# The last group's downward product: a bank of its own for the third step, the last step in two halves

## The chip, the cores and the metric

The kernel runs on one core of one Trainium2 chip. The metric is the device time of one execution in microseconds (us); of several runs the median is given.

## The reference

Attention with a sliding window and a few global keys gives 3072 tokens of 512 numbers. A router sends each token to one of 8 experts, and the expert's two-layer network makes the output. Only the second half matters here:

```python
logits = x @ w_gate                      # x: 3072 x 512, w_gate: 512 x 8
expert_idx = np.argmax(logits, axis=1)
gate_w = probs[np.arange(N), expert_idx]
for e in range(E):
    mask = expert_idx == e
    h = np.maximum(x[mask] @ w1[e], 0.0)     # 512 -> 1024
    out[mask] = gate_w[mask, None] * (h @ w2[e])   # 1024 -> 512
```

Everything is float32.

## The kernel before, in words

The attention writes each token's row, with its gate and its number, to a region of DRAM per expert. The experts then run as groups, in the order 0, 8 (the late tokens of expert 0), 1, ..., 7. `group(p)` records the work of a group. Group 7 is the last, and the only one that the change touches.

A group has up to 512 tokens, in two halves of up to 256. TensorE (PE) multiplies the weights, as stationary operand, by tokens, as moving operand; the number of moving columns is chosen at run time among 17 forms (128 to 256), and PE branches into the code of one form (L277, `emit_forms`). In the runs here the last group takes the form with 136 columns. Each layer is done by Strassen's scheme in Winograd's form: `seven` returns seven products, with sums on VectorE (DVE) and copies on ScalarE (ACT) around them. A product of the downward layer is 8 matmuls of 128x128 by 128x136; each leaves two records in the profile[...].

`seven` works with PSUM banks. There are two sets of three banks, `(0, 1, 2)` and `(3, 4, 7)`, which alternate from call to call: X, Y, W are this call's, X2, Y2, W2 those of the other set. Banks 6 and 5 (`tbanks`, handed out in turn by `bank()`) take the transposes of the output. The downward call of the last group (`half` given) runs its steps in the order one, two, four, five, six, three, last:

- `one`: b11 x a11 into X; ACT copies it to p1 (L898).
- `two`: t2 x s[1] into Y; DVE makes u2 = p1 + Y (L902).
- `four`: t3 x s[2] into Y; DVE makes u3 = u2 + Y (L913).
- `five`: t1 x s[0] into W; DVE makes c22 = u3 + W (L929).
- `six`: t4 x a22 into Y; DVE makes c21 = u3 + Y (L934).
- `three`: b21 x a12 added into X; ACT copies X to c11 (L909). In its middle `half()` turns and gates the blocks 1 and 3, which c21 and c22 complete.
- `last`: b22 x s[3] added into W; DVE makes c12 = u2 + W (L939).

`y_out` turns a block of 128 tokens with four transposes on PE (L849), one for each tile of 128 outputs, scales it by the gates on ACT (L852) or DVE (L854) into `self.y[j]`, and sends the rows to their places in the output with an indirect DMA of GpSimd (POOL, L860). Tiles 0 and 1 of blocks 0 and 2 come from c11, tiles 2 and 3 from c12. Blocks 1 and 3 are sent from within the program of the groups. Blocks 0 and 2 of the last group are turned and gated after it (L1404, L1405) and sent later, after a branch that every engine takes:

```python
    with tc.If(f.loads["redo"] > 0):      # L1801: a general version, for inputs outside the limits
        ...
    for j in (0, 2):
        d = ex.send(nc.gpsimd, order[-1], j)
```

Ahead of this branch SyncE (SP) collects a signal from every engine, and answers with one that POOL waits for before the sends (L216, `play`). The branch skips the general version's code.

`Flow` records operations in the order in which they are called, which is the order on each engine, and derives the semaphores: a PSUM bank is guarded as a whole, so a product into a bank waits for every earlier reader of it. The waits are put ahead of an instruction by L238.

Of the kernel before, what the change touches and what calls it, by code (L numbers as in the profile page):

```python
# [16 lines left out]
AF = mybir.ActivationFunctionType  # L17
ALU = mybir.AluOpType
# [644 lines left out]
class Experts:  # L663
# [163 lines left out]
    def bank(self):  # L827
        self.tp ^= 1
        return self.psum[:, self.tbanks[self.tp], :].rearrange("p (c t) -> p c t", c=4)
# [12 lines left out]
                lambda: V.tensor_tensor(sx[:, 2], a11, a21, ALU.subtract),  # L842
                lambda: V.tensor_tensor(sx[:, 3], a12, sx[:, 1], ALU.subtract)]

    def y_out(self, g, j, on="act", send=True):
        f, k, pt = self.f, self.keep, self.bank()
        hh, bb = (j % 2, j // 2) if g != self.E else (0, j)
        for c in range(4):
            f.pe.transpose(pt[:, c, :], self.yt[:, c, hh, ts(bb, 128)], k["ident"][:])  # L849
        y = self.y[j].rearrange("p (c t) -> p c t", c=4)  # L850
        if on == "act":
            f.act.activation(y, pt, AF.Copy, bias=0.0, scale=k["gt"][:, g, j, 0:1])  # L852
        else:
            f.dve.tensor_scalar(y, pt, k["gt"][:, g, j, 0:1], None, ALU.mult)  # L854
        if send:
            self.send(f.pool, g, j, _r=[k["to"][:, g, j:j + 1], self.y[j]], _w=[f"out{g}.{j}"])

    def send(self, pool, g, j, **kw):

# [13 lines left out]
            if half and t == 0:  # L873
                half()

    def seven(self, c, a, s, cols, order, dst, act, half=None, common=False):


        f, V = self.f, self.f.dve
        X, Y, W = self.sets[self.turn]  # L880
        X2, Y2, W2 = self.sets[self.turn ^ 1]
        some, past = slice(0, self.COMMON if common else 256), slice(self.COMMON, 256)
        p1, u2, u3 = self.p1[self.turn], self.u2[self.turn], self.u3[self.turn]
        self.turn ^= 1

        def bank(b):
            return self.psum[:, b, :].rearrange("p (t c) -> p t c", t=2)

        def mm(b, wq, xq, fresh, half=None, cut=slice(0, 256)):
            self.product(b, [c[wq][:, k, cols] for k in order], [xq[:, k, :] for k in order], fresh, half, cut)  # L890

        def relu(d):
            if act:
                f.act.activation(d, d, act)  # L894

        def one():
            mm(X, "b11", a["a11"], True, cut=some)
            f.act.copy(p1[:, :, some], bank(X)[:, :, some])  # L898

        def two():  # L900
            mm(Y, "t2", s[1], True, cut=some)
            V.tensor_tensor(u2[:, :, some], p1[:, :, some], bank(Y)[:, :, some], ALU.add)  # L902

        def three():
            mm(X, "b21", a["a12"], False, half, some)
            if act:
                f.act.activation(dst["c11"][:, :, some], bank(X)[:, :, some], act)  # L907
            else:
                f.act.copy(dst["c11"], bank(X))  # L909

        def four():
            mm(Y, "t3", s[2], True, cut=some)
            V.tensor_tensor(u3[:, :, some], u2[:, :, some], bank(Y)[:, :, some], ALU.add)  # L913

        def rest():
            T = self.tbanks[self.tp ^ 1]
            mm(X2, "b11", a["a11"], True, cut=past)
            f.act.copy(p1[:, :, past], bank(X2)[:, :, past])
            mm(Y2, "t2", s[1], True, cut=past)
            V.tensor_tensor(u2[:, :, past], p1[:, :, past], bank(Y2)[:, :, past], ALU.add)  # L920
            mm(W2, "b11", a["a11"], True, cut=past)
            mm(W2, "b21", a["a12"], False, cut=past)
            f.act.activation(dst["c11"][:, :, past], bank(W2)[:, :, past], act)
            mm(T, "t3", s[2], True, cut=past)
            V.tensor_tensor(u3[:, :, past], u2[:, :, past], bank(T)[:, :, past], ALU.add)

        def five():
            mm(W, "t1", s[0], True)
            V.tensor_tensor(dst["c22"], u3, bank(W), ALU.add)  # L929
            relu(dst["c22"])  # L930

        def six():
            mm(Y, "t4", a["a22"], True)
            V.tensor_tensor(dst["c21"], u3, bank(Y), ALU.add)  # L934
            relu(dst["c21"])

        def last():
            mm(W, "b22", s[3], False)
            V.tensor_tensor(dst["c12"], u2, bank(W), ALU.add)  # L939
            relu(dst["c12"])  # L940

        if half:
            return [one, two, four, five, six, three, last]
        if common:
            return [one, two, three, four, lambda: [rest(), five()], six, last]
        return [one, two, three, four, five, six, last]
# [24 lines left out]
    def down(self, e, half=None):  # L971

        c, h, yt = self.quarters(e, False), self.h, self.yt
        a = dict(a11=h[:, 0:4, 0], a12=h[:, 4:8, 0], a21=h[:, 0:4, 1], a22=h[:, 4:8, 1])
        s = [self.sh[:, j] for j in range(4)]
        dst = dict(c11=yt[:, 0:2, 0], c12=yt[:, 2:4, 0], c21=yt[:, 0:2, 1], c22=yt[:, 2:4, 1])
        return self.seven(c, a, s, slice(0, 256), (0, 1, 2, 3), dst, None, half)


    def plain(self, e, slack):  # L980
# [23 lines left out]
def kernel(  # L1004
# [51 lines left out]
    ident, iota_p, col, before, ones, rev8, ebase, base_e, tokid = (  # L1056
        keep[nm] for nm in ("ident", "iota_p", "col", "before", "ones", "rev8", "ebase", "base_e", "tokid"))
# [7 lines left out]
    with ExitStack() as stack:  # L1065
# [6 lines left out]
        f = Flow(tc)  # L1072
# [3 lines left out]
        ex = Experts(f, dict(moe_w1=moe_w1, moe_w2=moe_w2, xs=xg_dram, XW=XW, REGION=NTOK, out=out), psum, keep,  # L1076
                     (Arena(big, 0, WSET), Arena(big, WSET, WSET)), Arena(big, 2 * WSET, 22560 - 2 * DM), small[:, 0:XW], ylast[:])
        N, V = at.N, f.dve
# [25 lines left out]
        whole, half = slice(0, NBLK), NBLK // 2  # L1104
# [150 lines left out]
        order = [0, E, *range(1, E)]  # L1255
# [145 lines left out]

        for p in range(len(order)):
            group(p)
        for j, on in ((0, "act"), (2, "dve")):  # L1404
            ex.y_out(order[-1], j, on, send=False)  # L1405
        landing = f.play(later={f"out{order[-1]}.{j}" for j in (1, 3)})


    def anything(ctx):
# [372 lines left out]
        with tc.manual_schedule(engines={PE}):  # L1782
            for j in range(XB - 1):
                gather(j)
            for j in range(2):
                fetch(j)
            x_in(0)
            for j in range(JT):
                up(j)
                if j + 1 < JT:  # L1790
                    x_in(j + 1)
                if j:
                    down(j - 1)
                if j + XB - 1 < JT:
                    gather(j + XB - 1)
                if j + 2 < JT:
                    fetch(j + 2)
            down(JT - 1)
# [44 lines left out]
```

## Time and profile before

| what | us |
|---|---|
| median of 3 runs | 501.79 (500.29 to 501.93) |
| the profiled execution's own time | 500.38 |
| its span, first to last instruction | 498.5 |
| PE busy / DVE busy / ACT busy / POOL busy | 474.9 / 356.1 / 173.2 / 164.7 |
| granted clock of PE, mean | 0.991 of full speed |

The profile is of one execution; times within it count from its first instruction. The 1.9 us between its span and its own time lie around the span. A busy PE is not PE at its peak. A row of the time-line that merges several records starts with the first and ends with the last. In the rows of a branch or a semaphore the letter q marks the engine's own queue, as in POOLq; these rows are not counted as busy.

The downward call of the last group begins at about 469 us; its last matmul starts at 483.74, the last gate ends at 486.53, the two last sends start at 488.03 and 489.31, their data have landed by 492.6, and the span ends at 498.5.

### The profile page before, as it was taken

The numbers are of one execution on the slowest core, as the hardware profiler recorded it, in microseconds if no ns is written. First come the engines' busy times: TensorE is split into PE (matmuls) and PEld (weight loads), VectorE is DVE, ScalarE is ACT, GpSimd is POOL, SyncE is SP. The second block draws the span as 40 slices with busy tenths as digits, with TensorE's granted clock in tenths as the row PEclk, the third lists the DMA queues.
The fourth block names the chain that finished last, engine by engine and source line by source line (L and its number), as shares of the span: only waits on it lengthen the run. The fifth ranks groups of instructions, "written<-read, shape, count | busy, mean of one in ns | idle before, by whom it ended". The sixth has DMA issues, their size and how long they took to land. (4 is left out here: it accounts for less than half of the span.)

```text
span 498.5 us, 10842 instructions
## 1 busy us (share of the span) xinstructions
PE 474.9 (95%) x4413; PEld 450.0 (90%) x4413; DVE 356.1 (71%) x646; ACT 173.2 (35%) x309; POOL 164.7 (33%) x192
## 2 busy tenths in 40 slices
PE   7999999999997999999999999999999999999990
PEld 6888878878886899999999999999999999999880
DVE  6466766897888883766876886877877667778830
ACT  5656555654654230323123223214213204303310
POOL 2653576567774053303013113204304303003011
PEclk9999999999999999999999999999999999999996
DMA  9999999997624438896874773756666568001000
GB/s 175 215 246 237 213 237 267 244 212 188 149 87 86 172 129 189 215 265 131 189 214 111 192 217 102 172 181 156 157 204 146 121 175 239 0 1 66 3 26 30
DMA packets 120093, 79.26 MB, mean 159 GB/s; under 512 B 86170, under 2 KB 103066, under 8 KB 120020
## 3 DMA queue, kind: packets, MB, share of 16 engines
q1 hardware_dynamic: 112482, 63.52, 56.4%
q0 software_dynamic: 6480, 14.45, 8.1%
q8 instruction: 52, 0.85, 0.7%
q10 hardware_dynamic: 1058, 0.26, 0.2%
q14 instruction: 21, 0.17, 0.1%
HBM read 61.39 MB, written 23.71 MB: 171 GB/s over the span
## 5 line engine op out<-in xcount | busy, mean ns | idle before, releaser
L870 PE MATMUL psum<-arena 128*128 128x208 f32 (+5 forms) x1776 | 290.8, 325 | 1.0 <-DVE arena L902 0.8
L870 PEld LDWEIGHTS psum<-arena 128*128 128x128 f32 x1776 | 285.5, 190 | 2.6 <-DVE arena L902 1.3
L860 POOL DMA_INDIRECT out_dram<-arena,to x16 | 22.5, 1403 | 171.9 <-ACT arena L852 147.2
L529 DVE TENSOR_TENSOR arena<-psum,arena 128x1024 f32<-128x1024 f32 x40 | 48.3, 1219 | 29.4 <-PE psum L519 29.4
L537 ACT ACTIVATE arena<-arena 128x1024 f32<-128x1024 f32 (+1 forms) x48 | 47.4, 988 | 47.5 <-DVE arena L529 40.2
L543 POOL TENSOR_TENSOR arena<-arena 128x512 f32<-128x512 f32 x40 | 51.9, 1300 | 30.9 <-ACT arena L537 30.5
L894 ACT ACTIVATE arena<-arena 128x512 f32<-128x512 f32 x48 | 30.2, 630 | 53.4 <-DVE arena L929 27.5
L519 PE MATMUL psum<-arena 64*128 64x128 f32 x704 | 46.4, 280 | 1.6 <-ACT arena L505 1.6
L519 PEld LDWEIGHTS psum<-arena 64*128 64x128 f32 x704 | 41.8, 187 | 5.2 <-issue 2.5
L556 PE MATMUL psum<-arena 128*64 128x128 f32 x704 | 43.7, 276 | 0.3 <-issue 0.3
L898 ACT COPY arena<-psum 128x512 f32<-128x512 f32 (+1 forms) x24 | 13.5, 561 | 81.8 <-PE psum L870 81.7
L556 PEld LDWEIGHTS psum<-arena 128*64 128x64 f32 x704 | 37.9, 137 | 2.9 <-issue 0.6
L783 POOL DMA_INDIRECT xg_dram<-small,pad x24 | 23.4, 975 | 50.9 <-ACT arena L907 40.0
L655 POOL DMA_INDIRECT xg_dram<-arena,slot_i x24 | 25.4, 1058 | 21.9 <-DVE arena L939 16.2
L913 DVE TENSOR_TENSOR arena<-arena,psum 128x512 f32<-128x512 f32 (+1 forms) x24 | 15.8, 659 | 23.3 <-PE psum L870 21.9
L939 DVE TENSOR_TENSOR arena<-arena,psum 128x512 f32<-128x512 f32 x24 | 16.5, 688 | 17.8 <-PE psum L870 17.8
L934 DVE TENSOR_TENSOR arena<-arena,psum 128x512 f32<-128x512 f32 x24 | 16.5, 688 | 14.7 <-PE psum L870 11.5
L929 DVE TENSOR_TENSOR arena<-arena,psum 128x512 f32<-128x512 f32 x24 | 16.5, 688 | 13.5 <-PE psum L870 12.6
L860 POOL DMA_INDIRECT out_dram<-ylast,to x17 | 17.0, 1000 | 21.0 <-ACT ylast L852 13.1
L741 DVE TENSOR_TENSOR arena<-arena 128x1024 f32<-128x1024 f32 x16 | 21.1, 1321 | 1.3 <-issue 1.1
L902 DVE TENSOR_TENSOR arena<-arena,psum 128x512 f32<-128x512 f32 (+1 forms) x24 | 15.7, 656 | 8.5 <-PE psum L870 8.0
L738 DVE TENSOR_TENSOR arena<-arena 128x1024 f32<-128x1024 f32 x16 | 19.4, 1211 | 1.9 <-DMA arena<-in_moe_w_dram 1.9
(162 smaller groups left out, 541.8 us busy)
## 6 DMA issues: line engine op xcount, KB each, us to landing
arena<-in_moe_w_dram SPq DMA_DIRECT2D x64, 512.0 KB
arena<-xg_dram SPq DMA_DIRECT2D x64, 128.0 KB
arena<-in_v_dram SPq DMA_DIRECT2D x24, 256.0 KB
arena<-in_q_dram SPq DMA_DIRECT2D x23, 256.0 KB
arena<-in_k_dram SPq DMA_DIRECT2D x23, 256.0 KB
xg_dram<-arena SPq DMA_DIRECT2D x2, 1032.0 KB
xg_dram<-arena,slot_i POOLq DMA_INDIRECT x24, 5.5
xg_dram<-small,pad POOLq DMA_INDIRECT x24, 8.2
```

The lines of the kernel that those rows point to most:

```text
L519: f.pe.matmul(self.psum[:, 2 * g + a, c:c + P], lhsT=kt[r, m, :], rhs=qt[r, m, :], start=True, stop=True, skip_group_check=True)
L529: f.dve.tensor_tensor(e, s, self.bias[:, g, :, 1:3, :].rearrange("p h k c -> p h (k c)"), ALU.add)
L537: f.act.activation(e, e, AF.Exp)
L543: f.pool.tensor_tensor(self.es[n % 3][:, g], e[:, :, 0:P], e[:, :, P:2 * P], ALU.add)
L556: f.pe.matmul(po[r, m, :], lhsT=self.v[(n - ab) % 6][:, 2 * m + a, :], rhs=self.e[n % 2][:, m // 2, 2 * a + m % 2, P * ab:P * ab + P], sta ...
L655: self.f.pool.indirect_dma_start(out=self.xs[:], out_offset=bass.IndirectOffsetOnAxis(ap=k["slot_i"][:, b % 2, u:u + 1], axis=0), in_=self ...
L738: return [lambda: V.tensor_tensor(c["t3"], c["b22"], c["b12"], ALU.subtract), lambda: V.tensor_tensor(c["t1"], c["b12"], c["b11"], ALU.sub ...
L741: lambda: V.tensor_tensor(c["t4"], c["b21"], c["t2"], ALU.subtract)]
L783: self.f.pool.indirect_dma_start(out=self.xs[:], out_offset=bass.IndirectOffsetOnAxis(ap=self.keep["pad"][:, g, j:j + 1], axis=0), in_=sel ...
L860: return pool.indirect_dma_start(out=self.out[:], out_offset=bass.IndirectOffsetOnAxis(ap=self.keep["to"][:, g, j:j + 1], axis=0), in_=sel ...
L870: f.pe.matmul(self.psum[:, bank, 256 * t + cut.start:256 * t + cut.stop], lhsT=w[k][:, ts(t, 128)], rhs=x[k][:, cut], start=(fresh and t = ...
L894: f.act.activation(d, d, act)
```

## The change

In the last group's downward call alone:

- `four_end` puts the product t3 x s[2] into X2, and DVE makes u3 from there.
- `five_end` is `five`, and DVE then adds W to u2 as well. `last_end` therefore needs nothing of W.
- `last_end` puts b22 x s[3] into two fresh banks, the first 128 outputs into Y2 and the second into W2. After the first half DVE adds 128x256; then the tiles 0 and 1 of blocks 0 and 2 are turned into the banks 6 and 5 and gated (block 0 on ACT, block 2 on DVE). After the second half DVE adds the other 128x256; the tiles 2 and 3 are turned into W and X2 and gated.
- `y_out` is split into `y_turn` and `y_gate`. The calls of `y_out` for blocks 0 and 2 after the groups go; their transposes now lie inside each of PE's 17 forms.

The sends stay where they were.

```diff
-    def y_out(self, g, j, on="act", send=True):
+    def y_out(self, g, j, on="act"):
+        pt = self.bank()
+        self.y_turn(g, j, pt, range(4))
+        self.y_gate(g, j, pt, slice(0, 4), on)
+        self.send(self.f.pool, g, j, _r=[self.keep["to"][:, g, j:j + 1], self.y[j]], _w=[f"out{g}.{j}"])
+    def y_turn(self, g, j, pt, tiles):
         hh, bb = (j % 2, j // 2) if g != self.E else (0, j)
-        for c in range(4):
+        for c in tiles:
+            self.f.pe.transpose(pt[:, c, :], self.yt[:, c, hh, ts(bb, 128)], self.keep["ident"][:])
+    def y_gate(self, g, j, pt, tiles, on):
+        f, gate = self.f, self.keep["gt"][:, g, j, 0:1]
+        y = self.y[j].rearrange("p (c t) -> p c t", c=4)[:, tiles]
...
+        def four_end():
+            mm(X2, "t3", s[2], True)
+            V.tensor_tensor(u3, u2, bank(X2), ALU.add)
+        def five_end():
+            five()
+            V.tensor_tensor(u2, u2, bank(W), ALU.add)
+        def last_end():
+            blocks = (0, "act"), (2, "dve")
+            first, second = [self.bank(), self.bank()], [self.psum[:, b, :].rearrange("p (c t) -> p c t", c=4)
+                                                         for b in (W, X2)]
+            for t, b in enumerate((Y2, W2)):
+                for k in order:
+                    f.pe.matmul(self.psum[:, b, 0:256], lhsT=c["b22"][:, k, ts(t, 128)], rhs=s[3][:, k, :],
+                                start=(k == 0), stop=True, skip_group_check=True, _dyn=True)
+                V.tensor_tensor(dst["c12"][:, t], u2[:, t], self.psum[:, b, 0:256], ALU.add)
+                if t == 0:
+                    for pt, (j, on) in zip(first, blocks):
+                        self.y_turn(end, j, pt, (0, 1))
+                        self.y_gate(end, j, pt, slice(0, 2), on)
+            for tile in (2, 3):
+                for pt, (j, on) in zip(second, blocks):
+                    self.y_turn(end, j, pt, (tile,))
+            for pt, (j, on) in zip(second, blocks):
+                self.y_gate(end, j, pt, slice(2, 4), on)
...
         if half:
-            return [one, two, four, five, six, three, last]
+            return [one, two, four_end, five_end, six, three, last_end]
...
         for p in range(len(order)):
             group(p)
-        for j, on in ((0, "act"), (2, "dve")):
-            ex.y_out(order[-1], j, on, send=False)
```

## The prediction

> **What bounds the kernel now.** I start with the page's head and its busy shares.
>
> ```profile
> span 498.5 us, 10842 instructions
> PE 474.9 (95%) x4413; PEld 450.0 (90%) x4413; DVE 356.1 (71%) x646; ACT 173.2 (35%) x309; POOL 164.7 (33%) x192
> ```
>
> TensorE (PE) is the bound of the whole span, but the change touches only the last downward stage, so I read the end. The time-line of the last 30 us, one engine at a time, shows the place where PE rests inside that stage (columns: start, length, engine, line, operation, tiles, shape, count, idle time before and what ended it):
>
> ```profile
> 470.73 1.96 PE L870 MATMUL psum<-arena 128*128 128x136 f32 x15
> 473.54 1.66 PE L870 MATMUL psum<-arena 128*128 128x136 f32 x12 [0.85 <-DVE arena L902]
> ...
> 472.80 0.69 DVE L902 TENSOR_TENSOR arena<-arena,psum 128x512 f32<-128x512 f32 x1
> 473.40 1.22 DVE L741 TENSOR_TENSOR arena<-arena 128x1024 f32<-128x1024 f32 x1
> ```
>
> The reader is to see that `two`'s sum (L902) reads bank Y from 472.80 to 473.49 and that PE starts `four`, which overwrites Y, only at 473.54. From there PE runs without a pause to the end of `last`. The end of the stage and the output:
>
> ```profile
> 481.35 0.75 DVE L854 TENSOR_SCALAR arena<-psum,gt 128x512 f32<-128x512 f32 x1 [1.26 <-PE psum L849]
> ...
> 482.38 0.97 POOL L860 DMA_INDIRECT out_dram<-arena,to  x1 [22.25 <-DVE arena L854]
> 483.66 0.98 POOL L860 DMA_INDIRECT out_dram<-arena,to  x1 [0.30 <-issue]
> ...
> 484.06 0.69 DVE L939 TENSOR_TENSOR arena<-arena,psum 128x512 f32<-128x512 f32 x1 [1.96 <-PE psum L870]
> 484.80 0.88 PE L849 MATMUL psum<-ident,arena 128*128 128x128 f32 x6 [0.56 <-DVE arena L939]
> 485.33 0.69 ACT L852 ACTIVATE ylast<-psum,gt 128x512 f32<-128x512 f32 x1 [2.54 <-PE psum L849]
> 485.78 0.75 DVE L854 TENSOR_SCALAR ylast<-psum,gt 128x512 f32<-128x512 f32 x1 [1.04 <-PE psum L849]
> 488.03 0.97 POOL L860 DMA_INDIRECT out_dram<-ylast,to  x1 [3.39 <-remote]
> 489.31 0.98 POOL L860 DMA_INDIRECT out_dram<-ylast,to  x1 [0.30 <-issue]
> ```
>
> The last gate ends at 486.53, yet the first of the last two sends starts at 488.03. Does the gate or POOL set that start? The chain that ended last, and the instructions of the branch (L1801), answer:
>
> ```profile
> 486.10 0.91 another core or an unknown queue
> 487.01 0.10 POOLq L1801
> 487.11 0.03 issue
> 487.14 0.04 POOLq L860
> ...
> L1801 POOLq EVENT_SEMAPHORE  x6: 17/30/43, 485.6 to 486.1; - x6
> L1801 POOLq COMPARE_BRANCH  x1: 50/50/50, 482.9 to 482.9; - x1
> L1801 SPq COMPARE_BRANCH  x1: 50/50/50, 486.8 to 486.8; - x1
> ```
>
> The chain never reaches the gate. POOL branches at 482.95, right after it has issued the send of block 3; nothing of its queue runs for 2.67 us; from 485.62 it works through bookkeeping of semaphores (one step of 0.97 us), is at the send's waits at 487.23 and starts at 488.03. The other way in, last gate 486.53, SP's collection of the engines' signals, SP's release at 486.74, was there 0.49 us sooner. So **two ways end close together, and POOL's is the later**: gate of block 3 (481.35) to branch to send. Behind the sends, POOL's final drain and the closing barrier follow:
>
> ```profile
> L1838 POOLq DRAIN  x3: 40/188/8636, 488.3 to 497.9; - x3
> ```
>
> **What the skill says.** Three places bear on this. "PSUM — Partial Sum Buffer", section "PSUM bank collisions raise a hardware error": a bank must be guarded as a whole between engines, not by address. The trace agrees with the cost of that: PE waits 0.85 us for L902's read of Y. "Runtime: NRT & Kernel Launch", section "Instruction fetch mechanics": a taken branch whose target lies outside the fetched pages forces a DMA fetch. The trace agrees: after L1801's branch the queues resume 2.67 (POOL), 2.93 (SP), 2.98 (ACT) and 3.24 us (DVE) later. "Perfetto Trace Analysis", section on SWDGE instructions: a POOL DMA's bar ends with the writing of descriptors, not with the data. Here the bar is 0.97 us and landing comes 3.4 us after issue.
>
> **The change part by part.**
>
> 1. `four` goes to X2. That bank's last readers belong to the upward stage and are long done. The last matmul of `two` starts at 472.41 and the first of `four` at 473.54: 1.13 us where the rhythm is 0.116, so 1.01 us goes. The first matmul after that wait also delays its successor by 0.10 (0.22 from start to start). Sum **1.11 us**. What is late next: `four` needs the second half of s[2] (L955, ended 472.18) and its own 5th record at 472.99: no wait, at most 0.06 for a satisfied one, as in `two` (0.175 once instead of 0.116). Range 1.05 to 1.11. Then u3's sum: PE would be ready for it at 474.58, DVE is in L741 until 474.62; nobody needs u3 before `five` ends at 476.4, so nothing.
>
> 2. `u2 + W` is a new DVE sum of 128x512: 0.69 by row L929, 0.60 from start to start behind another. It sits between c22 (shifted: 476.50) and c21, whose product ends for 478.29. It is over at 477.79, 0.50 ahead: no cost; without that cover, c21 and the turn of blocks 1 and 3 would be late by what exceeds 0.50.
>
> 3. With 1 and 2 all of `five`, `six`, `three`, the turns of blocks 1 and 3, their gates, POOL's two sends and POOL's branch move forward by 1.11: branch at 481.84. POOL's instructions, sends and descriptors are the same in number and order; one block jump goes (below 0.1). After the same 2.67 of fetch and the same 2.40 of bookkeeping and issue the send starts at 486.91 instead of 488.03, provided SP's release is in by 486.12 instead of 487.23.
>
> 4. The halves of `last`: no matmul more or less (8), no transpose more or less (8). New shapes: DVE sums of 128x256, estimate 0.42 from 128x512 (0.69), 128x416 (0.58) and 128x96 (0.255); DVE gate of 128x256, estimate 0.48 (0.75 less 0.27); ACT gate of 128x256, 0.38 to 0.45 by row L994 (0.384 for that shape). Shifted, `last` starts at 480.89 and half one ends at 481.82. Turns of tiles 0 and 1 need c11 (ACT copy, shifted end 481.67): just met. Four turns x 0.109 to 482.26, second half to 483.19, its sum 483.39 to 483.81, two turns of tile 2 within that cover, two of tile 3 from 483.87, DVE's gate 484.42 to **484.90**. Before: 486.53. This way shortens by 1.63, that is 0.52 more than step 1. It was not the later way, so the 0.52 is worth **nothing**: the release comes at 485.10, 1.0 us ahead of POOL.
>
> 5. PE's jump to the end of the form moves behind the last turns, where it was hidden under matmuls (481.8). Cost 0.30 by its row:
>
> ```profile
> L277 PEldq COMPARE_BRANCH  x13: 292/303/909, 252.4 to 481.8; - x13
> ```
>
> It lies beside the gate's 0.48 and in the 1.0 of slack: nothing.
>
> Sum: 1.11 less 0 to 0.06, and 0 to 0.1 back: **1.1 us** less, at the end of the span. In the profiled execution: 500.38 - 1.1 = 499.3. That execution stands 1.41 under the median of the runs (501.79); the four times known (500.29, 500.38, 501.79, 501.93) average 501.10, which gives 500.0, and the median gives 500.7. I take 500.2.
>
> Unknown costs, both sides: POOL's fetch after the branch. The placement of its code changes by an instruction or so. If the target fell into pages already there, POOL would gain at most until the release governs, step 4's 1.63 and the 0.49 together: 2.1 us. If it takes as long as the slowest seen (PE's 3.6), 0.95 is lost again: 0.15 gained.
>
> **The rivals.**
>
> - The gain of both ways counts, or the fetch shortens: 1.6 to 2.1 us, 499.0 to 499.5 against 501.1. For it: the diff works mostly on the gate's way. Against it: the chain goes through POOL.
> - Nothing arrives (about 501.1): POOL's branch, or the drain after it, is tied to something that doesn't move. For it: the drain of 8.6 us ends 4.3 us after the last data landed, and no view says what it waits for. Against it: every step from the gate of block 3 on follows its predecessor without slack.
> - Slower: PE's jump (step 5) now has no matmuls in front to hide it. If it costs a fetch as L1801's do (2.7 to 3.6), PE's signal comes at 483.9 + 3.6 = 487.5, the release at 487.7 and the send 0.5 us later than before: 501.6 against 501.1. It loses from about 3.1 us of jump on. Against it: 13 such jumps took 0.29 to 0.91, with a prefetch hint ahead of each. A second wait of that kind on the other engines' jumps would make it worse, to +1.6.
> - The change might not remove the wait at all, if X2 were still held: its last reader (L907 of the upward stage) ended at 465.39, those of Y2 and W2 (L934, L939) by 469.65, so no.
>
> **How the numbers follow.** POOL's way, 1.1 us: 0.66. More, 1.6 to 2.1: 0.17. Nothing: 0.09. Slower: 0.08. A difference of 0.3% (1.5 us) is about what a measurement of this kernel can tell from no change, and the runs shown spread over 1.6 us. The likeliest case, 0.22%, lies under that bound; because the median before is at the upper end of its times I give half of it to either side: faster 0.33 + 0.17 = 0.50, same 0.33 + 0.09 = 0.42, slower 0.08. The range goes from 2.1 off the mean of the four, less 0.3 of scatter (498.7), to no gain at the upper median (501.8).
>
> **What would show it.** Right: PE has no pause before `four`; the sends of blocks 1 and 3 start 1.1 us sooner; the last gates end about 484.9; the last two sends start about 486.9, again 5 us after POOL's branch; the chain still runs through POOL. Wrong: a pause ahead of the turns of blocks 1 and 3 (step 2), a send that starts right after SP's release (step 4 counts), a POOL fetch unlike 2.67, a jump of PE over 1 us.

## The result and the profile after

The changed kernel takes 500.18 us (median of 20 runs, 498.97 to 502.26) against 501.75 (20 runs) for the kernel before. The ratio is 0.9973, with a 95% interval of 0.9961 to 0.9985: 1.35 us less, between 0.75 and 1.96. Ratios and intervals, here and below, are worked out from the fast runs alone (executions more than 1.5% above the fastest are left out), and are not quotients of the medians, which lie 1.57 us apart here. The prediction was 1.1 us less.

The profiled execution of the kernel after took 502.08 us itself, at the upper end of its runs. It reached the last downward call 2.75 us later than the profiled execution before. The change edits nothing ahead of that point, and the point moves between executions of one and the same kernel: 472.31 here and 470.41 in a second profile of the kernel after; over the 14 profiles of this study, of all versions, it lies anywhere from 469.56 to 474.44. So I compare from a mark inside the stage. The mark is the start of the last group's first sum of the hidden layer on DVE, 469.56 before and 472.31 after; **the tail** is the time from there to the end of the span: 28.97 us before, 27.86 after, 1.11 less. To set a time of the profile after beside one of before, take 2.75 off.

The page's head and its busy shares:

```profile
span 500.2 us, 10823 instructions
PE 475.9 (95%) x4413; PEld 451.1 (90%) x4413; DVE 359.6 (72%) x649; ACT 173.6 (35%) x310; POOL 164.7 (33%) x192
```

PE has its 4413 records as before; DVE has 3 instructions more (one sum, and the last sum and gate in halves). The shares say nothing of the gain.

The time-line of PE (start, length, engine, line, operation, shape, count, idle time before and what ended it):

```profile
469.81 12.11 PE L876 MATMUL psum<-arena 128*128 128x136 f32 x102
...
486.61 0.44 PE L854 MATMUL psum<-ident,arena 128*128 128x128 f32 x2 [0.30 <-DVE arena L961]
```

The reader is to see one unbroken row from ahead of the mark to the turn of blocks 1 and 3: the pause of 0.85 us before `four` is gone. The only pause left is the 0.30 before the last two turns. The time-line of DVE:

```profile
475.55 0.69 DVE L908 TENSOR_TENSOR arena<-arena,psum 128x512 f32<-128x512 f32 x1
...
477.40 0.69 DVE L945 TENSOR_TENSOR arena<-arena,psum 128x512 f32<-128x512 f32 x1
...
479.86 0.68 DVE L950 TENSOR_TENSOR arena<-arena,psum 128x512 f32<-128x512 f32 x1
481.04 0.69 DVE L940 TENSOR_TENSOR arena<-arena,psum 128x512 f32<-128x512 f32 x1 [0.50 <-PE psum L876]
482.98 0.75 DVE L862 TENSOR_SCALAR arena<-psum,gt 128x512 f32<-128x512 f32 x1 [1.26 <-PE psum L854]
484.76 0.42 DVE L961 TENSOR_TENSOR arena<-arena,psum 128x256 f32<-128x256 f32 x1 [1.03 <-PE psum L959]
485.27 0.48 DVE L862 TENSOR_SCALAR ylast<-psum,gt 128x256 f32<-128x256 f32 x1
...
487.08 0.48 DVE L862 TENSOR_SCALAR ylast<-psum,gt 128x256 f32<-128x256 f32 x1 [0.53 <-PE psum L854]
```

L945 is u3 from the new bank, L950 the added sum u2 + W: after it DVE still waits 0.50 us for `six` before c21 (L940). The gate of block 3 starts at 482.98, on the clock of before at 480.23 against 481.35. The last gate ends at 487.56, that is 484.81 against 486.53. The time-line of POOL, the end of the chain, and the branch (now L1834):

```profile
484.01 0.97 POOL L866 DMA_INDIRECT out_dram<-arena,to  x1 [21.14 <-DVE arena L862]
485.29 0.97 POOL L866 DMA_INDIRECT out_dram<-arena,to  x1 [0.30 <-issue]
489.68 0.97 POOL L866 DMA_INDIRECT out_dram<-ylast,to  x1 [3.41 <-remote]
490.95 0.97 POOL L866 DMA_INDIRECT out_dram<-ylast,to  x1 [0.30 <-issue]
```

```profile
487.75 0.91 another core or an unknown queue
488.66 0.10 POOLq L1834
488.76 0.03 issue
488.80 0.04 POOLq L866
```

```profile
L1834 POOLq EVENT_SEMAPHORE  x6: 17/30/43, 487.3 to 487.7; - x6
L1834 POOLq COMPARE_BRANCH  x1: 50/50/50, 484.6 to 484.6; - x1
L1834 SPq COMPARE_BRANCH  x1: 50/50/50, 487.8 to 487.8; - x1
```

The sends of blocks 1 and 3 come 1.11 us sooner, the last two 1.10 sooner, and the chain still goes through POOL's bookkeeping after its branch, not through a gate. The last gate is over at 487.56 and SP's release in at 487.78; the first of the last sends starts only at 489.68. I read "remote" as the releaser of that send, behind which the profile names no engine, as POOL's own bookkeeping of semaphores; where SP's release decides, the releaser reads "SPq", as some experiments show.

### The profile page after: what moved, and what is told of

Read it like the earlier page. It is cut to its first block, busy times and chain, and to the rows that moved or that the text cites. A ratio compares the mean times of both kernels' runs of the same rounds, so it can differ in the third digit from the quotient of the medians.

```text
span 500.2 us, 10823 instructions
## 1 busy us (share of the span) xinstructions
PE 475.9 (95%) x4413; PEld 451.1 (90%) x4413; DVE 359.6 (72%) x649; ACT 173.6 (35%) x310; POOL 164.7 (33%) x192
## 5 line engine op out<-in xcount | busy, mean ns | idle before, releaser
L556 PE MATMUL psum<-arena 128*64 128x128 f32 x704 | 45.0, 281 | 0.3 <-issue 0.3
L556 PEld LDWEIGHTS psum<-arena 128*64 128x64 f32 x704 | 39.1, 140 | 2.9 <-issue 0.6
L940 DVE TENSOR_TENSOR arena<-arena,psum 128x512 f32<-128x512 f32 x24 | 16.5, 688 | 14.5 <-PE psum L876 14.3
L741 DVE TENSOR_TENSOR arena<-arena 128x1024 f32<-128x1024 f32 x16 | 22.9, 1429 | 1.3 <-issue 1.1
L738 DVE TENSOR_TENSOR arena<-arena 128x1024 f32<-128x1024 f32 x16 | 19.4, 1210 | 2.1 <-DMA arena<-in_moe_w_dram 2.1
```

Of the source, the lines that this page charges most:

```text
L556: f.pe.matmul(po[r, m, :], lhsT=self.v[(n - ab) % 6][:, 2 * m + a, :], rhs=self.e[n % 2][:, m // 2, 2 * a + m % 2, P * ab:P * ab + P], sta ...
L738: return [lambda: V.tensor_tensor(c["t3"], c["b22"], c["b12"], ALU.subtract), lambda: V.tensor_tensor(c["t1"], c["b12"], c["b11"], ALU.sub ...
L741: lambda: V.tensor_tensor(c["t4"], c["b21"], c["t2"], ALU.subtract)]
```

## Experiments

Two theories stood at the start. **P**: the end follows POOL's branch, which follows the gate of block 3, so only the new bank (and u2 + W, which lets the last step do without W) brings anything. **G**: the end follows the last gate, so the halves bring their share. All tails in us from the mark. "POOL's way" is worked out from each trace: start of POOL's branch, 0.05 for it (0.07 with the hint), the gap after it, and 2.40 from POOL's next instruction to the send. "Release's way" is SP's release plus 0.79. The 2.40 and the 0.79 are read from these same traces: the first is the same in all seven of before, after (twice) and experiments 1, 2, 5 and 7, the second is seen alone in experiment 6. Experiments 3 to 6 and 11 are one execution each, and only their traces are used. The names are those of the experiments below.

| kernel | mark | tail | POOL's branch | gap after it | last gate ends | SP's release | POOL's way | release's way | first of the last sends |
|---|---|---|---|---|---|---|---|---|---|
| before | 469.56 | 28.97 | 13.39 | 2.62 | 16.97 | 17.17 | 18.46 | 17.96 | 18.46 |
| after | 472.31 | 27.86 | 12.27 | 2.64 | 15.25 | 15.47 | 17.36 | 16.26 | 17.37 |
| after, again | 470.41 | 28.15 | 12.26 | 2.94 | 15.25 | 15.46 | 17.65 | 16.25 | 17.65 |
| 1 bank alone | 469.63 | 28.00 | 12.26 | 2.79 | 15.85 | 16.05 | 17.50 | 16.84 | 17.50 |
| 2 halves alone | 469.94 | 29.18 | 13.39 | 2.84 | 16.38 | 16.59 | 18.68 | 17.38 | 18.68 |
| 3 two passes more | 470.10 | 28.74 | 12.27 | 2.72 | 16.29 | 17.46 | 17.44 | 18.25 | 18.24 |
| 4 five passes more | 471.01 | 30.16 | 12.27 | 2.95 | 17.85 | 18.88 | 17.67 | 19.67 | 19.67 |
| 5 gate 3 twice | 469.58 | 28.65 | 13.02 | 2.68 | 15.25 | 15.46 | 18.15 | 16.25 | 18.15 |
| 6 without two sends | 472.85 | 26.23 | -12.08 | - | 15.25 | 15.46 | - | 16.25 | 16.25 |
| 7 outer halves | 472.02 | 27.41 | 11.91 | 2.55 | 15.18 | 15.39 | 16.91 | 16.18 | 16.91 |
| 9 hint | 469.72 | 26.73 | 12.40 | 0.43 | 15.25 | 15.46 | 15.30 | 16.25 | 16.24 |
| 10 hint, bank alone | 471.73 | 27.32 | 12.40 | 0.43 | 15.85 | 16.05 | 15.30 | 16.84 | 16.82 |

In every row the send starts at the later of the two ways, within 0.02 us. From that send to the end of the span it is 10.5 us in every row but that of experiment 6 (9.98).

**1. The bank alone.** `four_end` stays; `five_end`, `last_end` and the turns between the halves go.

```diff
-            return [one, two, four_end, five_end, six, three, last_end]
+            return [one, two, four_end, five, six, three, last]
...
+        for j, on in ((0, "act"), (2, "dve")):
+            pt = ex.bank()
+            ex.y_turn(order[-1], j, pt, range(4))
+            ex.y_gate(order[-1], j, pt, slice(0, 4), on)
```

> The change's first half alone: four goes to X2, but last adds into W and is summed, turned and gated whole, after the groups, as before. I measure the tail: from the first of the last group's h-sums on DVE (469.56 in the profile before, 472.31 in the profile after) to the end of the span. It was 28.97 us before and is 27.86 after. Theory P (the end follows POOL's branch, which follows the gate of block 3): tail 27.86, all of the gain, although the last gate ends some 0.6 us later in the tail than after the whole change; time about 1.1 us under before. Rival G (the end follows the last gate): tail about 28.47, half of the gain.

Measured: 501.06 us (22 runs) against 502.58 (43 runs), ratio 0.9975 (0.996 to 0.9991): 1.26 us less, between 0.45 and 2.01. The tail is 28.00. From the time-lines of DVE and of POOL:

```profile
484.73 0.75 DVE L862 TENSOR_SCALAR ylast<-psum,gt 128x512 f32<-128x512 f32 x1 [1.04 <-PE psum L854]
```

```profile
487.13 0.97 POOL L866 DMA_INDIRECT out_dram<-ylast,to  x1 [3.56 <-remote]
```

The last gate ends 0.60 later from the mark than in the kernel after (15.85 against 15.25), yet the send is only 0.13 later, and the gap after POOL's branch is 0.15 longer (2.79 against 2.64). P holds: the bank brings the whole gain.

**2. The halves alone.** `four` goes back to Y.

```diff
-            return [one, two, four_end, five_end, six, three, last_end]
+            return [one, two, four, five_end, six, three, last_end]
```

> The change's second half alone: four goes to Y as before, so PE waits for the sum of two; the last product is in halves in two banks, with the turns and gates between. Theory P: tail 28.97 as before, no gain, though the last gate ends 0.6 us sooner. Rival G: tail about 28.36, a gain of 0.6 us.

Measured: 501.61 us (22 runs) against 502.58, ratio 0.9984 (0.9959 to 1.0009): no difference that these runs could tell. The tail decides: 29.18, as long as before plus the 0.22 by which the gap after POOL's branch is longer. From the time-lines of PE and of POOL:

```profile
473.91 4.32 PE L876 MATMUL psum<-arena 128*128 128x136 f32 x35 [0.85 <-DVE arena L908]
```

```profile
488.62 0.97 POOL L866 DMA_INDIRECT out_dram<-ylast,to  x1 [3.62 <-remote]
```

With `four` in Y the pause of 0.85 is back to the hundredth. The release comes 0.58 sooner than before (16.59 against 17.17) and nothing follows from it: G falls here, since it wanted 28.36.

**3. Two more passes of the last DVE gate**, to eat up the slack of the gate's way without touching POOL's.

```diff
             for pt, (j, on) in zip(second, blocks):
-                self.y_gate(end, j, pt, slice(2, 4), on)
+                for _ in range(1 if on == "act" else 3):
+                    self.y_gate(end, j, pt, slice(2, 4), on)
```

> The changed kernel, with the last gate of block 2 (128x256 on DVE, 0.48 us, 0.40 from start to start) computed three times in a row, to the same result: the last gate and SP's release come 0.8 us later. Theory P: the release still comes 0.3 us ahead of POOL, tail 27.86 as after the change. Rival G: tail 28.66.

Measured: tail 28.74, not 27.86. The time-lines of DVE and of POOL:

```profile
484.87 1.52 DVE L862 TENSOR_SCALAR ylast<-psum,gt 128x256 f32<-128x256 f32 x3 [0.53 <-PE psum L854]
```

```profile
488.34 0.97 POOL L866 DMA_INDIRECT out_dram<-ylast,to  x1 [4.30 <-SPq L216]
```

My size was wrong, not the theory. Each pass waits for the one before it and costs 0.52, so the gate ends 1.04 later; and the release then came 1.17 us after the gate's end, where it is 0.22 in the kernel after. Between them stands DVE's jump to the end of the form, which has a record of 0.05 us but after which DVE's queue came back only 1.3 us later. So the release moved by 1.99, past POOL's way (17.44 against 18.25), and the send started 0.78 after it. The releaser now reads "SPq L216": this is what a send that waits for the gates looks like.

**4. Five more passes**, well past the slack.

```diff
-                self.y_gate(end, j, pt, slice(2, 4), on)
+                for _ in range(1 if on == "act" else 6):
+                    self.y_gate(end, j, pt, slice(2, 4), on)
```

> The same with the last gate of block 2 computed six times: 2.0 us later. Theory P: the slack of 1.08 is used up and the release becomes the later way; tail 27.86 + 2.0 - 1.08 = 28.8. Rival G: tail 29.86. If the end hung on neither: 27.86.

Measured: tail 30.16, again more than expected, and for the same two reasons: the release moved by 3.41, to 18.88.

```profile
490.68 0.97 POOL L866 DMA_INDIRECT out_dram<-ylast,to  x1 [5.72 <-SPq L216]
```

The send starts 0.79 after it. From experiment 3 to this one release and send both move by 1.42 to 1.43: once the release is the later way, the end follows it one for one. Of the 3.41, the tail shows 2.30; the kernel after therefore had 1.11 to spare, against the 1.10 between its two ways in the table.

**5. The gate of block 3 twice**, in the kernel after: the other way in made longer.

```diff
-        self.y_gate(g, j, pt, slice(0, 4), on)
+        for _ in range(2 if on == "dve" else 1):
+            self.y_gate(g, j, pt, slice(0, 4), on)
```

> The changed kernel, with the gate of block 3 (128x512 on DVE) computed twice in a row, to the same result. DVE is idle for about 1.0 us behind it, so the second pass delays only POOL's send of block 3 and its branch, by 0.67 us. Theory P: tail 27.86 + 0.67 = 28.53. Rival G: tail 27.86, since the gates of blocks 0 and 2 don't move.

Measured: tail 28.65, 0.79 longer. The second pass waits for the first and costs 0.75; POOL's branch moves from 12.27 to 13.02, and the gap after it is 0.04 longer. The last gate ends at 15.25 in both.

```profile
487.73 0.97 POOL L867 DMA_INDIRECT out_dram<-ylast,to  x1 [4.18 <-remote]
```

The same engine and the same kind of instruction cost 0.75 here at full price and in experiment 3 were free up to the slack. That is P.

**6. Without the sends of blocks 1 and 3**, so that POOL reaches its branch long before.

```diff
         self.y_gate(g, j, pt, slice(0, 4), on)
+        if g == 7:
+            return
```

> The changed kernel without the two sends of blocks 1 and 3 of the last group: those rows of the output are not written. POOL has then nothing to wait for ahead of its branch and goes through it long before. Theory P, with its second part (behind POOL's way stands SP's release, some 1.05 us sooner): the first of the last two sends starts about 0.8 us behind SP's release instead of 1.9, tail 26.8. Rival G, or an end that hangs on something else than POOL's branch: tail 27.86.

Measured: tail 26.23; the first of the last sends starts at 16.25. From the instructions of the branch and the time-line of POOL:

```profile
L1836 POOLq COMPARE_BRANCH  x1: 50/50/50, 460.8 to 460.8; - x1
```

```profile
489.10 0.97 POOL L868 DMA_INDIRECT out_dram<-ylast,to  x1 [25.69 <-SPq L216]
```

With POOL out of the way the release governs, and its price of 0.79 from release to send is seen alone. The tail is 0.57 shorter than I expected, as from send to end it is 9.98 instead of 10.5. POOL's final drain took 8.47 us instead of 8.63, and the rest lies behind the drain; why two sends less shorten them isn't shown.

**7. The outer blocks' turns in halves as well**, so that the gate of block 3 ends sooner: `six_end` turns and gates tiles 2 and 3 of blocks 1 and 3 right after c21, `three_end` the tiles 0 and 1 where `half()` stood.

```diff
-            return [one, two, four_end, five_end, six, three, last_end]
+            return [one, two, four_end, five_end, six_end, three_end, last_end]
...
+        def six_end():
+            six()
+            self.early = [self.bank(), self.bank()]
+            for pt, (j, on) in zip(self.early, ((1, "act"), (3, "dve"))):
+                self.y_turn(end, j, pt, (2, 3))
+                self.y_gate(end, j, pt, slice(2, 4), on)
```

> A version meant to be faster by theory P: the changed kernel, and the blocks 1 and 3 are now treated as the change treats 0 and 2. Their tiles 2 and 3 (from c22) are turned right behind six and gated in halves of 128x256, their tiles 0 and 1 (from c21) are turned after three of the four matmuls of three's first half, into Y2 and W2. The gate of block 3 ends about 0.65 us sooner, block 1's about 0.4 sooner, and POOL issues the second send at best 0.55 behind the first: branch and end 0.38 us sooner. Theory P: tail 27.48. Rival G: 27.86 (the gates of blocks 0 and 2 stay).

Measured: 501.19 us (22 runs) against 502.86 (43 runs), ratio 0.9973 (0.9956 to 0.999); tail 27.41. POOL's branch is 0.36 sooner than in the kernel after and the gap 0.09 shorter, and the tail is 0.45 shorter. Halves pay where they stand ahead of the branch. The time itself can't be told from that of the kernel after.

**8. The kernel after a second time**, in the same comparison, unchanged.

> The changed kernel once more, on the same chip as the version before it, for a comparison of the two and for a second profile: tail 27.86 if it does not depend on the execution; the time about 1.1 us under before.

Measured: 501.74 us (22 runs) against 502.86, ratio 0.9987 (0.9965 to 1.0009); tail 28.15. Every time up to POOL's branch repeats within 0.01 us, but the gap after the branch was 2.94 instead of 2.64. The gain in the tail is 0.82 here, and by these runs alone it could also be none at all.

**9. A hint for POOL's branch**, set ahead of all of POOL's work (0.7 us into the span), some 480 us before the branch. If the gap is the fetch of the target's instructions, it should go, and the release become the later way. First one execution, then 22 against 43 of the kernel before:

```diff
+        self.tc.mark_branch_hint_location("redo", "LikelyTaken", [mybir.EngineType.Pool])
...
-    with tc.If(f.loads["redo"] > 0):
+    with tc.If(f.loads["redo"] > 0, label="redo"):
```

> The changed kernel with a prefetch hint for POOL's branch at L1834, set at the start of POOL's program, as PE's forms have one for their jump (0.30 us each in the profile). Theory P: if the hint is used, the 2.6 to 2.9 us between POOL's branch and its next instruction shrink to about 0.3, SP's release becomes the later way, the first of the last two sends starts 0.79 us behind the release (16.25 us into the tail instead of 17.37), and the tail is 10.5 more, 26.75. If the hint is lost over POOL's other jumps: 27.9 to 28.15, as the two executions of the changed kernel.

> The changed kernel with the prefetch hint for POOL's branch, timed against the version before the change. Theory P: tail 26.73 again, 2.24 us shorter than before and 1.1 shorter than after the change; time about 2.2 us under before, ratio 0.9955. If the hint costs something in the 470 us ahead of the tail (its one execution reached the tail late, at 474.44), the ratio stays at 0.997 or above.

Measured in the one execution: gap 0.43 instead of 2.64, tail 26.73 (it took 503.10 in all, but had reached the mark only at 474.44). Then: 499.67 us (22 runs, 497.75 to 505.87) against 502.07 (43 runs), ratio 0.9951 (0.9933 to 0.9968): 2.46 us less, between 1.61 and 3.36; the tail, 26.73 again, is 2.24 shorter than before. This is faster than the kernel before. It was not run beside the kernel after; there the tails tell, 26.73 against 27.86 and 28.15. Its branch, its send, and the end of its chain:

```profile
L1835 POOLq EVENT_SEMAPHORE  x6: 17/30/43, 482.6 to 483.1; - x6
L1835 POOLq COMPARE_BRANCH  x1: 68/68/68, 482.1 to 482.1; - x1
```

```profile
485.96 0.97 POOL L867 DMA_INDIRECT out_dram<-ylast,to  x1 [2.29 <-SPq L217]
```

```profile
482.57 0.94 PE psum L960 x8
483.51 0.02 issue
483.53 0.43 DVE arena L962
483.97 0.04 issue
484.01 0.45 PE psum L855 x2
484.46 0.02 issue
484.49 0.06 DVE ylast L863
484.55 0.15 issue
484.70 0.31 DVEq L217
485.01 0.02 issue
485.03 0.03 SPq L217
...
485.18 0.03 POOLq L867
```

Now, as in experiments 3, 4, 6 and 10, where the release is the later way too, the chain that ended last goes back through SP's release and the last gate, here to the second half of the product (L960); in the kernels before and after it doesn't.

That the gap is a fetch was so far read from its length. The record of the DMA queues shows the transfer itself. From POOL's branch to its next instruction in the kernel before (482.95 to 485.62):

```profile
q0 software_dynamic: 160, 0.28, 29.0%
q14 instruction: 1, 0.01, 1.5%
```

One transfer of instructions (8 KB) lies in the gap, starting about 1 us after the branch; the same is found in every kernel here without the hint. With the hint, from the branch to 1.78 us after it (482.12 to 483.90), there is none:

```profile
q0 software_dynamic: 79, 0.26, 39.3%
```

Another cause can be left out with it: POOL writes the descriptors of block 3's send while its queue rests, but with the hint it does so too (from 482.69 to 483.66), and its queue is back at 482.62.

**10. The hint with the bank alone**: what are the halves worth when POOL is not in the way?

> The hint on the version with the change's first half alone (four in X2, last whole). Theory P: SP's release now is the later way, it comes at 16.05 into the tail instead of 15.46, the send 0.79 behind it at 16.84, tail 27.33: the halves of last, worth nothing without the hint, are worth 0.6 us with it. If the halves had no worth even then: 26.73.

Measured: 500.25 us (22 runs) against 502.07, ratio 0.9973 (0.9955 to 0.9991); tail 27.32. The halves are worth 0.59 us in the tail with the hint, as the release comes 0.59 sooner with them. Without it they are worth nothing: experiment 1 differs from the kernel after by 0.14, and POOL's gap by 0.15.

**11. The other block of the branch as fall-through**, another try at the same gap.

```diff
-    with tc.If(f.loads["redo"] > 0):
+    with tc.If(f.loads["redo"] > 0, preferred_fallthrough_block=False):
```

> The changed kernel with the branch at L1834 laid out the other way round: the way that is taken here falls through to its own bookkeeping and jumps to the sends after it. The fetch then comes behind POOL's bookkeeping is issued (some 0.6 us) and beside the step of 0.97 us. Theory P: POOL is ready about 0.9 us sooner than after the change, SP's release is then about as late, first of the last sends 16.3 to 16.6 into the tail instead of 17.37, tail 26.8 to 27.1. If the end did not hang on POOL's fetch: 27.86 or more.

Measured: tail 27.83, mark 470.10; I had expected 26.8 to 27.1. The instructions of its branch on POOL:

```profile
L1834 POOLq EVENT_SEMAPHORE  x6: 17/30/43, 482.5 to 482.9; - x6
L1834 POOLq COMPARE_BRANCH  x2: 33/39/45, 482.4 to 484.0; - x2
L1834 POOLq INC_SWDGE_SEM  x1: 963/963/963, 483.0 to 483.0; - x1
```

The bookkeeping follows its compare without a gap, but POOL then meets a second jump at 483.98 (13.88 from the mark), and its queue comes back 2.54 us after that, again with one transfer of instructions in the gap. The fetch was moved, not removed; the send starts at 17.33, 0.04 sooner than in the kernel after.

## Why the prediction was right, point by point

- **Step 1, PE's wait.** 1.11 was forecast. POOL's branch came at 12.27 instead of 13.39, 1.12 sooner. What I named as late next (the second half of s[2], u3's sum) showed no wait. The prediction leans here on the Trainium skill, "PSUM — Partial Sum Buffer", section "PSUM bank collisions raise a hardware error", whose rule is a little finer than it says: guard by bank and quadrant of 32 partitions, by bank as the simple version. The step doesn't hang on that, since `four` overwrites the very columns that the sum of `two` still reads, so that a guard by address would make it wait too. Experiment 2 measures it a second time: same bank again, same 0.85.
- **Step 2, the added sum.** 0.50 us of cover was forecast; DVE idles 0.50 after it. Its price is nothing.
- **Step 3, POOL's branch and fetch.** 2.67 from the start of the branch to POOL's next instruction was carried over unchanged; measured 2.69. That it is a fetch was inferred then; experiment 9 shows it. This is the term that I treated as too firm: across the kernels whose POOL has this miss the gap after the branch was 2.54 to 2.95, and 2.64 and 2.94 for one and the same kernel. The forecast of the tail is right to 0.01 in the first profile (1.11) and 0.28 too large in the second (0.82); the difference is this term.
- **Step 4, the halves.** The last gate was forecast at 484.90, 15.34 from the mark; it ended at 15.25. The two DVE estimates (0.42 and 0.48) were met exactly; the gate on ACT took 0.47, just over its 0.38 to 0.45, but ended before DVE's (487.44 against 487.56). The release came at 15.47 where 15.54 was forecast, and the slack to POOL's way is 1.10 where 1.0 was. That this is worth nothing was argued then; experiments 1, 2 and 10 show it: without the halves the gain is there, the halves alone bring none, and with POOL's gap gone they bring their 0.59.
- **Step 5, PE's jump.** It took 0.303 us at 486.6, beside the last gate; its row (shortest, median and longest in ns):

```profile
L277 PEldq COMPARE_BRANCH  x13: 293/307/1409, 255.2 to 486.6; - x13
```

- **The rivals.** "Both ways count" is ruled out by experiments 1 and 2, its other half, a shorter fetch, by the 2.69. "Nothing arrives" is ruled out by the tail, and what I had not understood there, POOL's final drain, moves with the sends: in the kernel after it is again 8.63 us long (8629 ns, L1871), starting 0.3 us after the first of the last two sends, as before.

```profile
L1871 POOLq DRAIN  x3: 40/188/8629, 490.0 to 499.6; - x3
```

  "Slower" needed a last jump of PE of 3.1 us; it took 0.30, though another of the 13 took 1.41, more than the 0.91 of before. The mechanism does exist, though on another engine: in experiments 3 and 4 DVE's jump cost it over 1 us, and it decided once the release was late already.
- **The time.** 500.2 was forecast and 500.18 measured, and that is partly luck: the median of the first three runs before (501.79) was close to that of 20 (501.75), and not the mean of four that I leaned on. The ratio's 1.35 us is 0.24 more than the tail of the profiled pair; it lies well within the interval. The whole time can't confirm the forecast more closely than that: experiment 8 gave 0.65 us less for the same kernel, with an interval that includes no gain. What confirms it is the tail.

What stays open: why POOL's gap varies by 0.4 us between executions and builds, what fills the 1.0 to 1.4 us of it between the end of the transfer of instructions and POOL's next instruction, and what sets the 8.63 us of the final drain. I could only show that it moves with the last two sends.

## What to carry to other kernels

When two ways lead into one end, first find the later one and how much later it is; a change to the other way is worth nothing, however much shorter it gets, until the first is moved. The releaser in the row of the waiting instruction told which it was here ("remote" where POOL's own way was later, "SPq" where the release was), and so did the engine that the chain of waits goes back through. A branch near the end of a program belongs in that sum with what follows it, not with the 0.05 us of its record: 2.6 us here. A hint early in the program took 2.2 of them away; 1.1 of these reached the end of the kernel, before the other way became the later one.

## What the hardware showed that I had not expected

- **A hint works over a long time.** It was given some 480 us before the branch, with all of POOL's work and nine other branches of its queue between, and still the gap after it was 0.43 us instead of 2.54 to 2.95. Three profiles show it. How the target is kept ready isn't shown: no transfer of instructions is recorded in the first 12 us, where the hint stands.
- **The other queues' gaps grew by a half.** Without `last_end` (before, experiments 1 and 10) ACT came back 2.8 to 3.2 us after its branch, and PE's branch has a record of 3.5 to 3.9 us. With it (after, and the experiments built on it that leave the branch's layout alone) ACT took 3.8 to 4.8, and PE's record is 4.5 to 5.4. In those kernels the branches of the four queues mostly lie within 0.65 us instead of 1.0; but in experiments 3 and 4 DVE and SP branched 2 and 3.4 us later, and ACT still took 4.4 and 4.2. So that they crowd each other isn't shown. The record of the DMA queues has a candidate that no experiment tested: in the kernels with `last_end` PE's jump to the end of its form stands right ahead of its branch, and two transfers of instructions of 16 KB (q8) lie in that stretch instead of one, the longer of them taking 1.2 to 2.8 us. The cause is open. It costs nothing here, because POOL's drain ends later.
- **The same jump had two prices.** DVE's jump to the end of the form was over in 0.2 us in the kernel after and in experiment 5, and cost 1.2 to 1.3 in experiments 3 and 4, where two and five more gates stood right ahead of it; its record reads 0.05 us in every case. Why is open.
- **Passes over one destination.** A gate of 128x256 that waits for the gate before it costs 0.52 us from start to start where one alone takes 0.48; for 128x512 it was 0.75.
